# Where the negated head sums stand beside g_h, a smaller head mask, and how the gradient of z reaches all partitions

## The chip, the cores and the metric

The kernel runs on one core of a Trainium2 chip. A core has a matrix engine (TensorE, PE in the profile, with its weight loads PEld), a vector engine (DVE), a scalar engine (ACT), GpSimd (POOL) and a queue engine (SyncE, SP), and 16 DMA engines that all queues share. The metric is the device time of one execution in microseconds; lower is better.

## The reference, cut to what matters

A block of linear attention (no causal mask) with 32 heads of 20 columns (S = 2048 rows, D = 640 columns), followed by a gated MLP with F = 1728, and the gradients of both with respect to the input and all five weights:

```python
def _A_ref(x, wqkv, wo):              # x: [1, 2048, 640], H = 32 heads of Dh = 20
    q, k, v = split(x @ wqkv)
    phi = lambda t: jnp.where(t > 0, t + 1, jnp.exp(t)) + 1e-6
    pq, pk = phi(q), phi(k)
    kv = jnp.einsum("bhsd,bhse->bhde", pk, v)
    z = jnp.einsum("bhsd->bhd", pk)                      # sum of pk over the rows
    num = jnp.einsum("bhqd,bhde->bhqe", pq, kv)
    den = jnp.einsum("bhqd,bhd->bhq", pq, z)[..., None] + 1e-6
    return merge(num / den) @ wo
h  = x + _A_ref(_layernorm(x), A_wqkv, A_wo)
h2 = h + (silu(n @ w1) * (n @ w3)) @ w2                  # n = _layernorm(h)
out, vjp = jax.vjp(...);  grads = vjp(grad_out)          # x, wqkv, wo, w1, w3, w2
```

With r = pq / den, the backward pass needs, for each row and head, sn = the sum over the head's 20 columns of (gradient of num / den) times r. The gradient of z is then a 640-vector: for column d of head h, the sum over all rows of r[row, d] times -sn[row, h]. It is added to the gradient of pk in every row.

## The kernel before, in words

Everything is on one core, in an order written out by hand (a manual schedule; each engine and each DMA queue takes its instructions in program order). Rows are cut into 16 tiles of 128 (`ST = 16`, index t), the 640 columns into 5 blocks of 128 (`DT = 5`, index m). Blocks of 128 columns don't end where heads of 20 columns end: `M_H[m]` is the range of heads that block m touches, (0, 7), (6, 13), (12, 20), (19, 26), (25, 32).

The stages in order of time: the forward attention, the MLP with its backward products, the gradient of w2, then five that matter here.

- The gradient of the MLP's input. For each t, `b_ghn` (L1062) is 54 matmuls; `ln_bwd` (L1077) takes the layer norm's gradient on ACT and DVE and writes row tile t of `g_h`; `b_gT` (L1104) transposes it, `b_gr` (L1120) multiplies by the transposed wo into `gr`, and DVE forms `pb` = gr * r (L1131), sums it by head into `sn` (L1132) and writes -sn as bfloat16 into the 32 columns that stand behind the 640 of `g_h` in the tile `g_hx` (L1133). POOL spreads -sn over the columns of Zb into `sz` (L1135), and `b_gq` (L1137) makes `g_q` from it on DVE.
- `q_parts` (L1143, matmuls at L1155): for each m, r's column block m (the weights) times `g_h` (moving), in two halves j of 320 columns, each summed over 16 row tiles in one PSUM bank. The second half takes 352 columns, so that the 32 columns of -sn are multiplied too; out of these 32 only the heads of block m matter. A list `order` cuts each half into two parts of 8 row tiles; the caller places parts between the last `b_gr` and `b_gq` (L1223 to L1252). At the end of a block m, ACT copies the 640 columns to `qp`, DVE masks the 7 or 8 columns of block m's heads into `gz8` (L1160), and SP transposes `qp` into `QT` (both are parts of the tile `tri`). After the last one DVE sums `gz8` into `gz`, 128 partitions by 5: the gradient of z (L1253).
- `grad_halves` (L1265), shown as `job`: the products for the gradient of wqkv, 16 matmuls of 320 columns each. They are used as filling (`fill(n)`) between short dependent steps. The `q` part's results are written out by POOL's queue.
- The small square products: `gkvT` (L1322) from QT, masked by `masked` (L208); `dwoT`; then five rounds of `square` into `gm` (L1352) with transposes of `gkvT` and one `fill` each. In the first round DVE makes five diagonal 128 x 128 matrices `gzd` from the identity and `gz` (in the tile `small`, L1360). After the fifth, five matmuls of a matrix of ones with these diagonals (L1364) put the 640 values of `gz` on every partition, and two ACT copies (L1367) bring them to `gzb` (128 x 640, float32).
- The gradient of k, for each t: ten matmuls into `dkv` (L1375), DVE adds `gzb` into `gp` (L1378) and multiplies by pk's derivative (L1379). Then the gradient of x (`gxn`, L1429) and those of w1 and w3 (`job` again).

`mask` (L196) holds ones where partition p of block m belongs to head h, repeated over the head's 20 columns: 5 x 8 x 20 bfloat16, 1600 bytes on each partition. `make_mask` (L198) fills it with one DVE memset and two POOL selections for each m while the forward attention runs; `masked` multiplies with it at L211 (eight times in all).

SBUF tiles come from stacks. `mask` lies in the lowest pool, `cp`, that lives to the end, so the tiles of the pools above it, `u1`, `u2` and `bl` (x, all weights, g_h, r, g_q, g_k and so on), start at addresses that depend on its size; those of the other side (`pf`, `ph`, `pa`, `ba`, `br`) do not.

Of the kernel before, what the change touches and what calls it, by code (L numbers as in the profile page):

```python
# [9 lines left out]
P = 128  # L10
BF16 = mybir.dt.bfloat16
F32 = mybir.dt.float32
ALU = mybir.AluOpType
# [5 lines left out]
S, D, H, F = 2048, 640, 32, 1728  # L19
DH = D // H  # L20
ST, DT = S // P, D // P
# [3 lines left out]
HD = D // 2  # L25
# [4 lines left out]
def _heads(lo, hi, g):  # L30
    return lo // g, (hi - 1) // g + 1
# [3 lines left out]
M_H = [_heads(m * P, (m + 1) * P, DH) for m in range(DT)]  # L35
M_MAX = max(b - a for a, b in M_H)
# [19 lines left out]
def kernel(  # L56
# [19 lines left out]
    V, A, T, G, SY = nc.vector, nc.scalar, nc.tensor, nc.gpsimd, nc.sync  # L76
    dma, dmaT, dmaG = SY.dma_start, SY.dma_start_transpose, G.dma_start
# [12 lines left out]
    dram = ctx.enter_context(tc.tile_pool(name="dram", bufs=1, space=bass.MemoryType.DRAM))  # L90
# [5 lines left out]
    w_d = dram.tile([D, D], BF16, name="w_d")  # L96
    kvT_d = dram.tile([D, D], BF16, name="kvT_d")
    dwoT_d = dram.tile([D, D], BF16, name="dwoT_d")
    hn_d = dram.tile([S, D], BF16, name="hn_d")
    hh_d = dram.tile([F, S], BF16, name="hh_d")  # L100
    gg_d = dram.tile([2 * F, S], BF16, name="gg_d")
# [2 lines left out]
    def pool(name, side="left", space=None):  # L104
        kw = dict(space=space) if space is not None else dict(side=side)
        return tc.alloc_tile_pool(name=name, bufs=1, reuse_waits="tile", **kw)

    cp = pool("cp")
# [8 lines left out]
    ident = cp.tile([P, P], BF16, name="ident")  # L117
    make_identity(nc, ident[:])
    ones = cp.tile([P, P], BF16, name="ones")
# [8 lines left out]
    Zb = cp.tile([P, D], BF16, name="Zb")  # L128
# [64 lines left out]
    load_x(3, 4)  # L193
    load_x(4, 8)

    mask = cp.tile([P, DT, M_MAX, DH], BF16, name="mask")  # L196

    def make_mask(m):  # L198
        a, b = M_H[m]
        v = mask[:, m, 0:b - a, :]  # L200
        V.memset(v, 1.0)

        G.affine_select(out=v, in_=v, pattern=[[-DH, b - a], [0, DH]], compare_op=ALU.is_ge, fill=0.0,
                        base=m * P - a * DH, channel_multiplier=1)
        G.affine_select(out=v, in_=v, pattern=[[DH, b - a], [0, DH]], compare_op=ALU.is_gt, fill=0.0,
                        base=a * DH + DH - m * P, channel_multiplier=-1)

    def masked(out, acc, m):  # L208

        a, b = M_H[m]  # L210
        V.tensor_tensor(out=out[:, m, a * DH:b * DH].rearrange("p (h e) -> p h e", e=DH),  # L211
                        in0=acc.rearrange("p (h e) -> p h e", e=DH), in1=mask[:, m, 0:b - a, :], op=ALU.mult)


    w1 = U2.tile([P, DT, FP], BF16, name="w1", tag="A")
# [64 lines left out]
    def two(ap):  # L280
        return ap.rearrange("p (j n) -> p j n", j=2)
# [78 lines left out]
    def heads(ap):  # L360
        return ap.rearrange("p (h e) -> p h e", e=DH)
# [555 lines left out]
    for c in range(SC):  # L917
# [9 lines left out]
        for fc in range(FT):  # L927
# [8 lines left out]
            if c == 0 and fc in (5, 7, 9, 11):  # L936
                a, b = {5: (0, 3), 7: (3, 6), 9: (6, 10), 11: (10, 13)}[fc]
# [12 lines left out]
            if c == SC - 1 and fc in (1, 2, 5, 6):  # L950
                i = (1, 2, 5, 6).index(fc)
# [66 lines left out]
    for fc in range(FT - 1):  # L1018
        b, i = divmod(fc, 4)
        if fc == FT - 2:  # L1020
            gw2_tail()
        acc = ps.tile([P, 2, 512], F32, name="gw", bufs=4)
        for j in range(2):
            for t in range(ST):
                T.matmul(acc[:, j, 0:HD], lhsT=hb[b][:, t, i * P:(i + 1) * P], rhs=g2[:, t, j * HD:(j + 1) * HD],  # L1025
                         start=(t == 0), stop=(t == ST - 1))
# [15 lines left out]


    bl = pool("bl")
    g_hx = bl.tile([P, ST, D + H], BF16, name="g_h")
    g_h = g_hx[:, :, 0:D]
    g_q = bl.tile([P, ST, D], BF16, name="g_q")
    bo = pool("bo")
    r_sb = bo.tile([P, ST, D], BF16, name="r_sb")
    ps = pool("pbp", space=PSUM)  # L1050

    gz8 = cp.tile([P, DT, 8], F32, name="gz8")
    V.memset(gz8[:], 0.0)
    gz = cp.tile([P, DT], F32, name="gz")
# [60 lines left out]
    gr, cc, sz = {}, {}, {}  # L1115

    def per_head(ap):
        return ap.unsqueeze(2).to_broadcast([P, H, DH])

    def b_gr(t):  # L1120

        cc[t] = br.tile([P, D], F32, name="cc")
        V.tensor_tensor(out=heads(cc[t][:]), in0=heads(r_sb[:, t, :]), in1=per_head(rden[:, t, :]), op=ALU.min)
        gr[t] = ps.tile([P, 2, 512], F32, name="gr", bufs=2)
        for j in range(2):
            for c in range(DT):
                T.matmul(gr[t][:, j, 0:HD], lhsT=ghT[t][:, c, :], rhs=wT2[:, c, j * HD:(j + 1) * HD], start=(c == 0),  # L1127
                         stop=(c == DT - 1))
        pb = br.tile([P, D], F32, name="pb")
        sn = br.tile([P, H], F32, name="sn", bufs=2)  # L1130
        V.tensor_tensor(out=two(pb[:]), in0=gr[t][:, :, 0:HD], in1=two(r_sb[:, t, :]), op=ALU.mult)  # L1131
        V.reduce_sum(out=sn[:], in_=heads(pb[:]), axis=AX.X)  # L1132
        V.tensor_scalar(out=g_hx[:, t, D:], in0=sn[:], scalar1=-1.0, scalar2=None, op0=ALU.mult)  # L1133
        sz[t] = br.tile([P, D], F32, name="sz")
        G.tensor_tensor(out=heads(sz[t][:]), in0=heads(Zb[:]), in1=per_head(g_hx[:, t, D:]), op=ALU.mult)  # L1135

    def b_gq(t):  # L1137
        V.tensor_tensor(out=two(sz[t][:]), in0=gr.pop(t)[:, :, 0:HD], in1=two(sz[t][:]), op=ALU.add)
# [4 lines left out]
    def q_parts():  # L1143

        acc = {}
        tags = ("ghn", "ghn", "gr", "ghn", "ghn")
        order = [(0, 0, 0), (0, 0, 1), (1, 0, 0), (1, 0, 1), (0, 8, 0), (1, 8, 0), (2, 0, 0), (2, 0, 1), (0, 8, 1),
                 (1, 8, 1), (2, 8, 0), (2, 8, 1)]
        order += [(m, t0, j) for m in (3, 4) for t0 in (0, 8) for j in range(2)]
        for m, t0, j in order:  # L1150
            if m not in acc:
                acc[m] = ps.tile([P, 2, 512], F32, name="gwo", tag=tags[m], bufs=2)
            n = HD + H * j
            for t in range(t0, t0 + 8):
                T.matmul(acc[m][:, j, 0:n], lhsT=r_sb[:, t, m * P:(m + 1) * P],  # L1155
                         rhs=g_hx[:, t, j * HD:j * HD + n], start=(t == 0), stop=(t == ST - 1))
            if (t0, j) == (8, 1):
                a, b = M_H[m]
                A.copy(out=two(qp[:, m, :]), in_=acc[m][:, :, 0:HD])
                V.tensor_tensor(out=gz8[:, m, 0:b - a], in0=acc.pop(m)[:, 1, HD + a:HD + b], in1=mask[:, m, 0:b - a, 0],  # L1160
                                op=ALU.mult)
                dmaT(out=QT[:, :, m * P:(m + 1) * P], in_=qp[:, m, :])
            yield
# [18 lines left out]
    for t in range(ST):  # L1182
# [14 lines left out]
        if t >= 1:  # L1197
# [3 lines left out]
            if t <= 2 * DT:  # L1201
                n = (t - 1) % DT
# [5 lines left out]
        if u >= 0:  # L1208
            b_gr(u)
# [10 lines left out]
    QT, qp = (tri[:, k * DT:(k + 1) * DT, :] for k in range(2))  # L1220
# [6 lines left out]
    a, b = ST - 1, ST - 2  # L1227
# [23 lines left out]
    load_xnT(2)  # L1251
    part(20)  # L1252
    V.reduce_sum(out=gz[:], in_=gz8[:], axis=AX.X)  # L1253


    OB = DT * D
# [39 lines left out]
    def d_acc():  # L1296
        return ps.tile([P, 2, 512], F32, name="dkv", bufs=3)
# [9 lines left out]
    def unload(acc, out):  # L1307
        for bank, (a, b) in enumerate(((0, SPLIT_D), (SPLIT_D, H))):
            (A.copy, V.tensor_copy)[bank](out=out[:, a * DH:b * DH], in_=acc[:, bank, 0:(b - a) * DH])

    def fill(n):
        for _ in range(n):
            next(jobs, None)
# [4 lines left out]
    for m, (a, b) in enumerate(M_H):  # L1318
        n = (b - a) * DH
        acc = ps.tile([P, 512], F32, name="gkvT", tag="dkv", bufs=3)  # L1320
        for c in range(DT):
            T.matmul(acc[:, 0:n], lhsT=woT[:, c, m * P:(m + 1) * P], rhs=QT[:, c, a * DH:b * DH], start=(c == 0),  # L1322
                     stop=(c == DT - 1))
# [9 lines left out]
    pkT = bv.tile([P, DT, S], BF16, name="pkT")  # L1333
    small = bv.tile([P, ST, D], BF16, name="small", tag="hnN")
    mN, gkv_b, gm = (small[:, n:n + DT] for n in (0, DT, 2 * DT))
    gzd = small[:, 3 * DT, :].rearrange("p (m q) -> p m q", q=P)
    dma(out=mN, in_=m_v)
    dma(out=rows(dwoT_d), in_=dwoT[:])

# [4 lines left out]
        (dma if c < 4 else dmaG)(out=pkb[c][:], in_=pk_v[:, c * 2:(c + 1) * 2, :])  # L1344

    gzb = dx.tile([P, D], F32, name="gzb")
    g_k = gqkv[1] = U1.tile([P, ST, D], BF16, name="g_k", tag="S0")
    for n in range(4):
        load_pk(n)

    for i, (c, ms) in enumerate(SQ_BLOCKS):
        unload(square(wqT[:, 2 * DT:, :], gkvT, i), gm[:, i, :])  # L1352
        tr = ps.tile([P, len(ms), P], BF16, name="trk", tag="dkv", bufs=3)
        for k, m in enumerate(ms):
            T.transpose(tr[:, k, :], gkvT[:, m, c * P:(c + 1) * P], ident[:])
        V.tensor_copy(out=gkv_b[:, c, ms[0] * P:(ms[-1] + 1) * P].rearrange("p (i q) -> p i q", q=P), in_=tr[:])
        fill(1)
        if i == 0:
            for m in range(DT):
                V.tensor_scalar(out=gzd[:, m, :], in0=ident[:], scalar1=gz[:, m:m + 1], scalar2=None, op0=ALU.mult)  # L1360
        dmaT(out=wqT[:, 2 * DT:, i * P:(i + 1) * P], in_=gm[:, i, :])
    acc = d_acc()
    for m in range(DT):
        T.matmul(acc[:, m // 4, m % 4 * P:(m % 4 + 1) * P], lhsT=ones[:], rhs=gzd[:, m, :], start=(m % 4 == 0),  # L1364
                 stop=True, skip_group_check=True)
    for x, y, bank in ((0, 4 * P, 0), (4 * P, D, 1)):
        A.copy(out=gzb[:, x:y], in_=acc[:, bank, 0:y - x])  # L1367

    for t in range(ST):
        c, i = divmod(t, TPC)  # L1370
        u = t // 2
        acc = d_acc()
        for j in range(2):
            for k in range(DT):
                T.matmul(acc[:, j, 0:HD], lhsT=xnT[c][:, k, i * P:(i + 1) * P], rhs=gm[:, k, j * HD:(j + 1) * HD],  # L1375
                         start=(k == 0), stop=(k == DT - 1))
# [7 lines left out]
        if t in (2, 5, 8, 11, 14):  # L1384
            n = t // 3
            acc = square(mN, gkv_b, n)
# [8 lines left out]
        if t in (6, 8, 10, 12):  # L1395
            n = t // 2 - 3
# [110 lines left out]
```

## Time and profile before

| | |
|---|---|
| median of 3 runs | 823.8 us (823.18, 823.80, 824.32) |
| profiled execution, first to last instruction (span) | 821.9 us |
| profiled execution's own time | not recorded apart from the span; the median stands 1.9 us above the span |
| granted TensorE clock | 1.000 |
| PE busy | 814.4 us, 99% of the span, 5522 matmuls |
| DVE, ACT, POOL busy | 453.1, 325.0, 133.1 us |
| DMA | 157.26 MB, mean 191 GB/s |
| q_parts' matmuls (gwo, L1155) | 160, first 537.9, last 563.9 us |
| ones-matmuls for gzb (L1364) | 5, at 582.68 us |

A row of a timeline has the start in us, the time, the engine, the line, the operation, out<-in, how many, and in brackets the idle time before it with what ended it. Matmul durations there overlap (a 320-column matmul is shown with 299 ns, but one starts every 136 ns), so costs on PE are read from the chain of work that ended last, where a stretch of n matmuls has the time from the first start to the next one's. A share of 1.00 or more for DMA means that all 16 engines had packets all the time.

### The profile page before, as it was taken

The numbers are of one execution on the slowest core, as the hardware profiler recorded it, in microseconds if no ns is written. First come the engines' busy times: TensorE is split into PE (matmuls) and PEld (weight loads), VectorE is DVE, ScalarE is ACT, GpSimd is POOL, SyncE is SP. The second block draws the span as 40 slices with busy tenths as digits, with TensorE's granted clock in tenths as the row PEclk, the third lists the DMA queues.
The fourth block names the chain that finished last, engine by engine and source line by source line (L and its number), as shares of the span: only waits on it lengthen the run. The fifth ranks groups of instructions, "written<-read, shape, count | busy, mean of one in ns | idle before, by whom it ended". The sixth has DMA issues, their size and how long they took to land.

```text
span 821.9 us, 14179 instructions
## 1 busy us (share of the span) xinstructions
PE 814.4 (99%) x5522; PEld 522.6 (64%) x5549; DVE 453.1 (55%) x961; ACT 325.0 (40%) x609; POOL 133.1 (16%) x194
## 2 busy tenths in 40 slices
PE   8999999999999999999999999999999999999998
PEld 6677544555555555777777777767777777555554
DVE  7869887999898566300057777772681545200000
ACT  7856688665565666011122212222212334211111
POOL 2243333323223212100001111110220000000000
PEclk9999999999999999999999999999999999999999
DMA  9999889696485556999677897258984898885771
GB/s 233 254 279 227 207 234 312 196 242 157 145 213 155 166 181 162 250 241 267 195 170 179 206 204 188 70 113 178 268 216 93 164 200 181 201 199 137 165 170 38
DMA packets 320883, 157.26 MB, mean 191 GB/s; under 512 B 238704, under 2 KB 314064, under 8 KB 320816
## 3 DMA queue, kind: packets, MB, share of 16 engines
q1 hardware_dynamic: 278768, 115.54, 61.3%
q0 software_dynamic: 7328, 24.48, 8.9%
q10 hardware_dynamic: 34720, 16.34, 8.7%
q8 instruction: 43, 0.70, 0.4%
q14 instruction: 24, 0.20, 0.1%
HBM read 47.01 MB, written 51.13 MB: 119 GB/s over the span
## 4 chain that ended last, share of the span: by engine, by line
PE 94%; DVE 2%; ACT 1%; DMA 1%; issue 0%; SPq 0%; POOL 0%; DVEq 0%; ACTq 0%
PE mm L386 20%; PE job L1271 20%; PE ghn L1070 14%; PE gxn L1429 8%; PE o L833 7%; PE gw L1025 7%; PE gwo L1155 3%; PE big L266 3%; PE gr L1127 3%; PE dkv L1375 3%; PE macc L416 2%; PE at L642 2%; DMA wqkv<-in_A_wqkv_dram 1%; PE dkv L1303 1%; DVE st L147 1%; DMA Wp<-pkx 1%
## 5 line engine op out<-in xcount | busy, mean ns | idle before, releaser
L1271 PE MATMUL job<-gb,hnN 128*128 128x432 bf16 (+2 forms) x656 | 117.0, 342 | 0.0
L1070 PEld LDWEIGHTS <-ggb 128*128 128x128 bf16 x864 | 84.5, 98 | 32.8
L1271 PEld LDWEIGHTS <-hnN 128*128 128x128 bf16 x656 | 63.6, 98 | 53.4
L386 PE MATMUL mm<-pqT,w 128*128 128x512 bf16 x397 | 93.1, 379 | 0.5
L386 PEld LDWEIGHTS <-w 128*128 128x128 bf16 x540 | 52.5, 98 | 63.1 <-issue 0.8
L1275 ACT CAST obs<-job 128x432 bf16<-128x432 f32 (+3 forms) x61 | 29.3, 480 | 123.1 <-PE job L1271 123.1
L833 PE MATMUL o<-w,hhT 128*128 128x320 bf16 x448 | 67.7, 299 | 0.1
L1070 PE MATMUL ghn<-w13a,ggb 128*128 128x320 bf16 x448 | 63.5, 299 | 0.0
L1070 PE MATMUL ghn<-w13b,ggb 128*128 128x320 bf16 x416 | 61.4, 299 | 0.0
L386 PE MATMUL mm<-g2T,w2T 128*128 128x512 bf16 x227 | 58.5, 379 | 0.6
L833 PEld LDWEIGHTS <-hhT 128*128 128x128 bf16 x448 | 43.8, 98 | 23.8 <-issue 0.2
L1025 PE MATMUL gw<-g,hb 128*128 128x320 bf16 x416 | 56.8, 299 | 0.0
L1135 POOL TENSOR_TENSOR sz<-Zb,g_h 128x640 f32<-128x640 bf16 x16 | 20.2, 1260 | 198.8 <-DVE g_h L1133 107.7
L1025 PEld LDWEIGHTS <-hb 128*128 128x128 bf16 x416 | 40.6, 98 | 16.0 <-issue 0.3
L1429 PE MATMUL gxn<-wqT,gT 128*128 128x320 bf16 x320 | 48.7, 299 | 0.0
L406 ACT CAST ghh<-mm 128x512 bf16<-128x512 f32 x48 | 28.3, 590 | 44.7 <-PE mm L386 39.0
L772 ACT ACTIVATE sig<-mm 128x512 bf16<-128x512 f32 x56 | 33.9, 605 | 25.1 <-PE mm L386 21.6
L1082 ACT ACTIVATE gs<-ghn 128x640 bf16<-128x640 f32 x16 | 11.2, 703 | 78.9 <-PE ghn L1070 73.4
L386 PEld LDWEIGHTS <-w2T 128*128 128x128 bf16 x260 | 25.4, 98 | 23.3
L266 PEld LDWEIGHTS <-pqT 128*128 128x128 bf16 x320 | 30.6, 98 | 14.4 <-issue 1.7
L1429 PEld LDWEIGHTS <-gT 128*128 128x128 bf16 x320 | 31.3, 98 | 12.2
L266 PE MATMUL big<-wqkv,pqT 128*128 128x320 bf16 x250 | 38.5, 299 | 0.3
(210 smaller groups left out, 1282.3 us busy)
## 6 DMA issues: line engine op xcount, KB each, us to landing
hh_d<-hhT SPq DMA_DIRECT2D x24, 256.0 KB, 2.8
gg_d<-gate POOLq DMA_DIRECT2D x24, 256.0 KB, 4.1
gg_d<-ghh POOLq DMA_DIRECT2D x24, 256.0 KB, 3.5
ggb<-gg_d SPq DMA_DIRECT2D x6, 896.0 KB, 5.4
ggb<-gg_d ACTq DMA_DIRECT2D x6, 832.0 KB, 5.7
out_dram<-obs ACTq DMA_DIRECT2D x39, 108.0 KB, 3.0
x_sb<-in_A_x_dram SPq DMA_DIRECT2D x6, 640.0 KB, 5.4
ggb<-gg_d SPq DMA_DIRECT2D x2, 1728.0 KB, 13.5
```

The costliest lines, as they stand in the source:

```text
L266: T.matmul(acc, lhsT=pqT[:, c, t * P:(t + 1) * P], rhs=wqkv[:, c, n0:n0 + HD], start=(c == 0), stop=(c == DT - 1))
L386: T.matmul(acc[:], lhsT=w[:, c, fc * P:(fc + 1) * P], rhs=rhs[:, c, :], start=(c == 0), stop=(c == DT - 1))
L406: A.copy(out=ghh[n // 2][:, n % 2, :], in_=acc[:])
L772: A.activation(sig[:, i, :], gp[:], AF.Sigmoid)
L833: T.matmul(o2["ps"][:, 0:HD], lhsT=hhT[c][:, fc, i * P:(i + 1) * P], rhs=w2[:, fc, j * HD:(j + 1) * HD], start=(fc == 0), stop=(fc == FT - 1))
L1025: T.matmul(acc[:, j, 0:HD], lhsT=hb[b][:, t, i * P:(i + 1) * P], rhs=g2[:, t, j * HD:(j + 1) * HD], start=(t == 0), stop=(t == ST - 1))
L1070: T.matmul(acc[:, j, 0:HD], lhsT=ggb[t // 2][:, k, lo:lo + P], rhs=rhs[:, j * HD:(j + 1) * HD], start=(k == 0), stop=(k == NG - 1))
L1127: T.matmul(gr[t][:, j, 0:HD], lhsT=ghT[t][:, c, :], rhs=wT2[:, c, j * HD:(j + 1) * HD], start=(c == 0), stop=(c == DT - 1))
L1155: T.matmul(acc[m][:, j, 0:n], lhsT=r_sb[:, t, m * P:(m + 1) * P], rhs=g_hx[:, t, j * HD:j * HD + n], start=(t == 0), stop=(t == ST - 1))
L1271: T.matmul(acc[:, 0:n], lhsT=lhs[:, t, m * P:(m + 1) * P], rhs=rhs(t), start=(t == 0), stop=(t == ST - 1))
L1275: A.copy(out=ob, in_=acc[:, 0:n])
L1429: T.matmul(acc[:, j, 0:HD], lhsT=g, rhs=wqT[:, k, j * HD:(j + 1) * HD], start=(k == 0), stop=(k == 14))
```

## The change

- `g_hx` gets 16 columns ahead of `g_h`'s 640. The last 13 of them hold -sn of heads 19 to 31 (`n_hi` = 13), written by a second small DVE operation in `b_gr`, after the POOL operation has been queued; the 32 columns behind stay. One row is now 688 elements instead of 672.
- In `q_parts` blocks 0, 1 and 2 take -sn from behind g_h, and only as many columns as their heads reach (7, 13, 20) in the second half; blocks 3 and 4 take it from ahead of g_h (13, 7 columns) in the first half, and their second half has 320.
- `mask` loses the repetition over 20 columns: 80 bytes on each partition. `masked` reads it with a step of 0.
- The diagonals, the five matmuls with ones and the two copies are gone. POOL's queue writes `gz` to a small DRAM tensor `gz_d` (640 separate elements of 4 bytes) and later reads it back to all 128 partitions of `gzb` at once.

```diff
+    gz_d = dram.tile([DT, P], F32, name="gz_d")
...
-    mask = cp.tile([P, DT, M_MAX, DH], BF16, name="mask")
+    mask = cp.tile([P, DT, M_MAX], BF16, name="mask")
...
-        v = mask[:, m, 0:b - a, :]
+        v = mask[:, m, 0:b - a]
         V.memset(v, 1.0)
-        G.affine_select(out=v, in_=v, pattern=[[-DH, b - a], [0, DH]], compare_op=ALU.is_ge, fill=0.0,
+        G.affine_select(out=v, in_=v, pattern=[[-DH, b - a]], compare_op=ALU.is_ge, fill=0.0,
...
-                        in0=acc.rearrange("p (h e) -> p h e", e=DH), in1=mask[:, m, 0:b - a, :], op=ALU.mult)
+                        in0=acc.rearrange("p (h e) -> p h e", e=DH), in1=mask[:, m, 0:b - a].unsqueeze(2).to_broadcast([P, b - a, DH]),
+                        op=ALU.mult)
...
-    g_hx = bl.tile([P, ST, D + H], BF16, name="g_h")
-    g_h = g_hx[:, :, 0:D]
+    G0 = 16
+    g_hx = bl.tile([P, ST, G0 + D + H], BF16, name="g_h")
+    g_h, g_n = g_hx[:, :, G0:G0 + D], g_hx[:, :, G0 + D:]
+    n_hi = H - M_H[3][0]
...
-        V.tensor_scalar(out=g_hx[:, t, D:], in0=sn[:], scalar1=-1.0, scalar2=None, op0=ALU.mult)
+        V.tensor_scalar(out=g_n[:, t, :], in0=sn[:], scalar1=-1.0, scalar2=None, op0=ALU.mult)
         sz[t] = br.tile([P, D], F32, name="sz")
-        G.tensor_tensor(out=heads(sz[t][:]), in0=heads(Zb[:]), in1=per_head(g_hx[:, t, D:]), op=ALU.mult)
+        G.tensor_tensor(out=heads(sz[t][:]), in0=heads(Zb[:]), in1=per_head(g_n[:, t, :]), op=ALU.mult)
+        V.tensor_scalar(out=g_hx[:, t, G0 - n_hi:G0], in0=sn[:, H - n_hi:], scalar1=-1.0, scalar2=None, op0=ALU.mult)
...
-            n = HD + H * j
+            a, b = M_H[m]
+            up, lo = (0, H - a) if m > 2 else (b, 0)
+            x, y = (0, lo + HD) if j == 0 else (lo, lo + HD + up)
             for t in range(t0, t0 + 8):
-                T.matmul(acc[m][:, j, 0:n], lhsT=r_sb[:, t, m * P:(m + 1) * P],
-                         rhs=g_hx[:, t, j * HD:j * HD + n], start=(t == 0), stop=(t == ST - 1))
+                T.matmul(acc[m][:, j, x:y], lhsT=r_sb[:, t, m * P:(m + 1) * P],
+                         rhs=g_hx[:, t, G0 - lo + j * HD + x:G0 - lo + j * HD + y], start=(t == 0), stop=(t == ST - 1))
             if (t0, j) == (8, 1):
-                a, b = M_H[m]
-                A.copy(out=two(qp[:, m, :]), in_=acc[m][:, :, 0:HD])
-                V.tensor_tensor(out=gz8[:, m, 0:b - a], in0=acc.pop(m)[:, 1, HD + a:HD + b], in1=mask[:, m, 0:b - a, 0],
+                A.copy(out=two(qp[:, m, :]), in_=acc[m][:, :, lo:lo + HD])
+                z = acc.pop(m)[:, 0, 0:b - a] if m > 2 else acc.pop(m)[:, 1, HD + a:HD + b]
+                V.tensor_tensor(out=gz8[:, m, 0:b - a], in0=z, in1=mask[:, m, 0:b - a],
                                 op=ALU.mult)
...
     V.reduce_sum(out=gz[:], in_=gz8[:], axis=AX.X)
+    dmaG(out=gz_d[:, :].rearrange("m p -> p m"), in_=gz[:])
...
-    gzd = small[:, 3 * DT, :].rearrange("p (m q) -> p m q", q=P)
...
     gzb = dx.tile([P, D], F32, name="gzb")
+    dmaG(out=gzb[:], in_=gz_d[:, :].rearrange("m p -> (m p)").partition_broadcast(P))
...
-        if i == 0:
-            for m in range(DT):
-                V.tensor_scalar(out=gzd[:, m, :], in0=ident[:], scalar1=gz[:, m:m + 1], scalar2=None, op0=ALU.mult)
         dmaT(out=wqT[:, 2 * DT:, i * P:(i + 1) * P], in_=gm[:, i, :])
-    acc = d_acc()
-    for m in range(DT):
-        T.matmul(acc[:, m // 4, m % 4 * P:(m % 4 + 1) * P], lhsT=ones[:], rhs=gzd[:, m, :], start=(m % 4 == 0),
-                 stop=True, skip_group_check=True)
-    for x, y, bank in ((0, 4 * P, 0), (4 * P, D, 1)):
-        A.copy(out=gzb[:, x:y], in_=acc[:, bank, 0:y - x])
```

More of the change, by code (lines that the diff above doesn't have):

```diff
@@ L194 @@
     load_x(4, 8)
-    mask = cp.tile([P, DT, M_MAX, DH], BF16, name="mask")
+    mask = cp.tile([P, DT, M_MAX], BF16, name="mask")
     def make_mask(m):
         a, b = M_H[m]
-        v = mask[:, m, 0:b - a, :]
+        v = mask[:, m, 0:b - a]
         V.memset(v, 1.0)
-        G.affine_select(out=v, in_=v, pattern=[[-DH, b - a], [0, DH]], compare_op=ALU.is_ge, fill=0.0,
+        G.affine_select(out=v, in_=v, pattern=[[-DH, b - a]], compare_op=ALU.is_ge, fill=0.0,
                         base=m * P - a * DH, channel_multiplier=1)
-        G.affine_select(out=v, in_=v, pattern=[[DH, b - a], [0, DH]], compare_op=ALU.is_gt, fill=0.0,
+        G.affine_select(out=v, in_=v, pattern=[[DH, b - a]], compare_op=ALU.is_gt, fill=0.0,
                         base=a * DH + DH - m * P, channel_multiplier=-1)
```

## The prediction

> **What bounds the kernel now.** First the page: its busy times and its chain of what ended last. (About 0.2% of the time, 1.65 us here, is what a measurement of this kernel can tell from no change.)
>
> ```profile
> PE 814.4 (99%) x5522; PEld 522.6 (64%) x5549; DVE 453.1 (55%) x961; ACT 325.0 (40%) x609; POOL 133.1 (16%) x194
> ...
> PE 94%; DVE 2%; ACT 1%; DMA 1%; issue 0%; SPq 0%; POOL 0%; DVEq 0%; ACTq 0%
> ```
>
> PE is the bound, at a clock of 1.000, and idle for only 7.5 us. So what leaves PE in a dense stretch leaves the time, and what leaves DVE, ACT or POOL is worth nothing unless PE waits for it. Second, the chain in order of time, which gives what PE really pays for a matmul:
>
> ```profile
> 65.21 2.75 PE macc L416 x20
> ...
> 543.41 2.28 PE gwo L1155 x16
> 545.69 1.36 PE gr L1127 x10
> 547.04 17.15 PE gwo L1155 x120
> ...
> 613.03 15.21 PE job L1271 x112
> ```
>
> A 320-column matmul costs 15.21 / 112 = 0.1358 us. The 120 of gwo are 56 of 320 columns and 64 of 352: (17.15 - 56 x 0.1358) / 64 = 0.1492 us, so 32 columns more cost 13.4 ns, 0.417 ns a column, and the stretch holds no idle time. Third, the timeline of the same stretch, for those who come just in time:
>
> ```profile
> 542.95 0.28 PEld L1111 LDWEIGHTS <-g_h 128*128 128x128 bf16 x5 [0.19 <-DVE g_h L1095]
> ...
> 545.26 0.18 DVE L1133 TENSOR_SCALAR g_h<-sn 128x32 bf16<-128x32 f32 x1
> ...
> 545.58 1.26 POOL L1135 TENSOR_TENSOR sz<-Zb,g_h 128x640 f32<-128x640 bf16 x1 [6.60 <-DVE g_h L1133]
> 546.88 0.82 DVE L1138 TENSOR_TENSOR sz<-gr,sz 128x640 f32<-128x640 f32 x1 [1.44 <-POOL sz L1135]
> ...
> 551.04 0.18 DVE L1133 TENSOR_SCALAR g_h<-sn 128x32 bf16<-128x32 f32 x1
> ```
>
> Two gates: PE's transposes wait 0.19 us at 542.95 for DVE's last g_h, and the last -sn (row tile 15) is ready at 551.04 + 0.18 = 551.22. DVE runs without a gap from 538.96 but for the wait on POOL at 546.88, so PE can't hasten this.
>
> Fourth, the timeline where gzb is made, and the rows that price its replacement:
>
> ```profile
> 582.19 0.43 DVE L1309 CAST small<-dkv 128x260 bf16<-128x260 f32 x1 [0.90 <-ACT small L1309]
> ...
> 582.68 0.44 PE L1364 MATMUL dkv<-small,ones 128*128 128x128 bf16 x5
> ...
> 582.96 2.88 PE L1375 MATMUL dkv<-small,xnT 128*128 128x320 bf16 x20
> 583.20 0.76 ACT L1367 COPY gzb<-dkv 128x512 f32<-128x512 f32 x2
> ...
> 584.59 0.82 DVE L1378 TENSOR_TENSOR gp<-dkv,gzb 128x640 f32<-128x640 f32 x1 [1.77 <-PE dkv L1375]
> ```
>
> ```profile
> q1 hardware_dynamic: 278768, 115.54, 61.3%
> q0 software_dynamic: 7328, 24.48, 8.9%
> ```
>
> ```profile
> 564.95 1.20 SPq L1162 DMA_TRANSPOSE tri<-tri  x1
> 574.36 0.54 POOL L1276 DMA_DIRECT2D out_dram<-obs  x1 [4.52 <-ACT obs L1275]
> ```
>
> ```profile
> out_dram<-obs POOLq DMA_DIRECT2D x10, 80.0 KB, 4.4
> pkb<-pk_d SPq DMA_DIRECT2D x4, 320.0 KB, 7.3
> tri<-tri SPq DMA_TRANSPOSE x5, 2.6
> ```
>
> **Part 1, narrower gwo.** Before, 80 matmuls have 32 extra columns: 2560. After, the extra columns of blocks 0 to 4 are 7, 13, 20, 13, 7, in 16 row tiles each: 960. 1600 columns x 0.417 ns = 0.67 us less PE. Not all of it arrives. What is saved before 542.95 (block 0, rows 0 to 7: 8 x 25 columns, 0.08 us) ends in the wait for DVE's g_h, which only grows. Then block 1 (8 x 19 columns, 0.063), block 2 (8 x 12, 0.040) and the first seven of block 0's last part (7 x 25, 0.073) bring PE 0.176 us earlier to the matmul that reads the last -sn. Before, it came there at 546.88 + 16 x 0.1358 + 15 x 0.1492 = 551.29, 0.07 after DVE; after, at 551.11, so it waits until about 551.27. What is left is the rest: that matmul 0.010, block 1 0.063, block 2 0.040, block 3 (512 - 208 = 304 columns) 0.127, block 4 (512 - 112 = 400) 0.167, and 0.02 of margin used up: 0.42 us. The next to be late is the bank that block 3 takes from block 0: free when DVE has masked block 0, about 554.5, wanted at 554.78; no wait.
>
> **Part 2, the negative sums ahead of g_h.** 16 more DVE operations. Nearest rows: L1133 with 32 columns 0.18 us, one-column operations 0.15; I take 0.16, 2.6 us of DVE in all. Behind each on DVE stands either L1085, which waits 1.38 us for ACT, or L1138, which waits 1.44 us for POOL, and POOL's operation is queued ahead of it. Cost nothing; with that cover gone it would be 0.16 us per tile, of which PE would see only tile 14's at the 551.22 gate. That gate waits for L1133, not for the new operation.
>
> **Part 3, odd starts.** Blocks 3 and 4 now read moving columns that start 3 and 9 elements into a row. The nearest row is macc, whose rows of 1284 bytes start at every multiple of 4 bytes: 2.75 / 20 = 0.1375 us with a change of bank among them, against 0.1358. So nothing to 1.7 ns for each of 32 matmuls, below 0.06 us; I take nothing. An odd element is not shown by any row; if the read ran at half rate, the 32 matmuls would cost 16 x (333 + 327) x 0.417 ns = 4.4 us. The Trainium skill ("SBUF — State Buffer", Operand start alignment) says that a bfloat16 operand may start at any multiple of 2 bytes, and that this is about legality and nothing was timed.
>
> **Part 4, gzb by DMA.** PE loses five matmuls: 582.96 - 582.68 = 0.28 us, in a dense stretch, all of it on the path. Next late would be the last part of gm, from DVE at 582.19 + 0.43 = 582.62, before 582.68 and needed only by the fifth matmul: no wait. The two ACT copies (0.76) and five DVE operations (0.90 at 576.49) stood in idle time: nothing. On POOL's queue two DMAs are added. The first waits for gz (DVE, 565.36) and stands ahead of the job results at 567.13; the second stands behind the one at 574.36 and waits for the first to land. Behind both are only result stores, whose ring of ten buffers isn't full, and four pkb loads from 588.65 on. Landing of the second: issued about 574.9, and between 4.4 us (POOL's rows there) and 7.3 us (pkb of the same size at the same time, four in a row), so 579.3 to 582.2; DVE wants it when PE's first dkv is done, about 583.9 in the new time. Hidden with 1.7 us or more. Reading one short line for all partitions has no row.
>
> The first DMA is 640 elements of 4 bytes, 40 for each of 16 engines. Priced by the packet: q1 0.613 x 821.9 x 16 / 278768 = 0.029 us, q0 0.089 x 821.9 x 16 / 7328 = 0.160 us: 1.2 to 6.4 us on each engine from about 566 on. Size speaks for the low end: q0's packets carry 3.3 KB, q1's 0.4 KB. In that time the last transpose into QT (issued 564.95, 2.6 us, so there at 567.6) is due; gkvT's fourth block, at 568.38 + 15 x 0.062 = 569.3, needs it. The margin is 1.7 us: at the low end, hidden. A rule speaks against this part: the Trainium skill ("DMA: Bandwidth & Descriptors", Specifications) puts line rate at 512 bytes and up, with a read-modify-write below. It gives no time for it; if each write cost double the low end, an estimate of 2.4 us would be 0.7 over the margin and the sum 0.7 us later.
>
> **Part 5, mask and addresses.** POOL's ten selections (0.34 to 0.50 us) and DVE's five memsets (0.175) shrink at 42 to 49 us, with their first reader at 66.6: nothing. L211 reads its mask with a step of 0; L1123, which does that already, takes 0.82 us like L1131, which does not: nothing. All tiles of the lower pools move down by 1504 bytes, from 32 bytes past a 64-byte border onto one. What DMAs gain or lose by that, PE sees only where it waits for them: 1.2 us on wqkv at 6.6 and 8.1, and 0.8 us on Wp at 90. After the wqkv waits PE waits for DVE anyhow (L160, at 9.51). So between 0.8 us less (the Wp wait gone) and 0.8 more; I take 0.2 less, as a start on a border should not hurt.
>
> **Sum.** 0.42 + 0.28 + 0.2 = 0.9 us less, span 821.0. The profiled execution's own time is not given apart from its span; the median stands 1.9 us above, so 822.9.
>
> **The rivals.**
> 1. Faster by more than 1.65 us. The sure savings give 0.7; the -sn gate may open too (0.25 more), and the Wp wait and some of wqkv's go (1.0): 821.8. For it: every saving is PE's. Against: only 2.0 us of PE's waits are on DMA. 0.2.
> 2. Slower: the 4-byte writes hold back QT. At 6.4 us an engine instead of 1.2, with the transposes served in turn, QT lands up to 5 us late, 3.3 beyond the margin, in front of gkvT, with everything behind: 823.8 - 0.7 + 3.3 = 826.4. It decides from 1.7 us of lateness on, and for more than 1.65 us of loss from some 4. A late gzb would act alike, but PE has three dkv buffers of 1.4 us in hand there. 0.11.
> 3. Odd starts at half rate: 823.8 - 0.7 + 4.4 = 827.5. 0.03.
> 4. It doesn't pay: the gate at 551.22 or new waits of a few tenths eat part 1, and 0.28 is left: 823.5. 0.12.
>
> The forecast has 0.54. Within 0.2% lie the forecast and rival 4, 0.66; faster rival 1, 0.20; slower 2 and 3, 0.14. The range, 821.5 to 824.9, takes in the forecast, rival 4 and most of rival 1, and leaves out 2 and 3.
>
> **What would show it.** After: gwo in the chain x120 at about 16.6 us with PE idle for some 0.15 us on DVE's L1133 counterpart; no matmuls with ones, dkv following job directly; gp not waiting for DMA; no wait at gkvT; the odd blocks at 0.141 and 0.138 us a matmul. Wrong would be a wait of PE on tri or of DVE on gzb, matmuls near 0.28 us in blocks 3 and 4, or a difference that comes from before 500 us.

## The result, and the profile after

The changed kernel takes 834.05 us (median of 6 runs, 832.77 to 836.04) against 824.08 us for the kernel before (6 runs): a ratio of 1.0121, with an interval of 1.0108 to 1.0134. It is slower by 10 us where 0.9 us of gain was forecast, and lies outside the range. The profiled execution has a span of 833.3 us and a time of its own of 835.05 us, so 1.7 us lie outside the span. Its span is 11.4 us longer than that of before.

The page of the changed kernel, busy times, shares of the chain, and the granted clock in 40 slices of the span:

```profile
PE 818.5 (98%) x5517; PEld 525.9 (63%) x5544; DVE 453.0 (54%) x972; ACT 324.9 (39%) x607; POOL 132.8 (16%) x196
...
PE 95%; DMA 2%; SPq 1%; DVE 1%; ACT 0%; issue 0%; DVEq 0%
...
PEclk9999999999999999999999999997999999999999
```

There are five matmuls fewer, as the change says, yet PE is busy 4.1 us longer: something made matmuls slower, and one slice has a clock of 0.7. In the chain the share of DMA has gone from 1% to 2% and that of SP's queue from 0% to 1%. The chain in order of time shows where:

```profile
547.91 12.45 PE gwo L1162 x88
...
561.10 2.06 SPq L1169
...
565.95 12.52 DMA tri<-tri
...
578.51 1.34 PE gkvT L1330 x10
579.86 1.83 PE dkv L1311 x18
581.69 2.13 PE job L1279 x8
583.83 0.44 PE dkv L1311 x6
584.26 1.09 PE job L1279 x8
585.35 0.33 PE dkv L1311 x6
...
594.58 2.72 PE dkv L1374 x20
```

One transpose into `QT` (a part of `tri`) takes 12.52 us from issue to landing; the prediction's row for these had 2.6. The work behind it then runs at about half rate: eight matmuls of `job` take 2.13 us and, two lines on, 1.09. The chain leaves PE at 560 us because the transposes, not the matmuls, were what `gkvT` waited for.

The timeline (core 0, the same stretch), with the write that the change adds:

```profile
565.73 0.20 DVE L1260 TENSOR_REDUCE gz<-gz 128x5 f32<-128x40 f32 x1
565.95 1.22 SPq L1169 DMA_TRANSPOSE tri<-tri  x1
566.23 0.94 POOL L1261 DMA_DIRECT2D gz_d<-gz  x1 [12.67 <-DVE gz L1260]
...
568.95 1.12 PE L1330 MATMUL gkvT<-tri,woT 128*128 128x140 bf16 x15
...
578.51 1.34 PE L1330 MATMUL gkvT<-tri,woT 128*128 128x140 bf16 x10 [8.44 <-DMA tri<-tri]
```

POOL issues the 640 elements of `gz` at 566.23, between the issue of the last transpose and its landing. The first 15 matmuls of `gkvT` go through; the fourth block waits 8.44 us. The view of the DMA queues from 560 to 582 us gives the time to landing (KB of one, median us):

```profile
out_dram<-obs POOLq DMA_DIRECT2D x2, 80.0 KB, 12.3
...
gz_d<-gz POOLq DMA_DIRECT2D x1, 2.5 KB, 11.7
```

The 2.5 KB took 11.7 us, and the 80 KB job results on the same queue, which took 5.7 us in this stretch before, 12.3 us. The transposes on SP's queue are held up too, so it is not only POOL's queue. The windows (stretch, its length, then busy time of PE, PEld, DVE, ACT and POOL with the number of instructions; the last three numbers are granted clock, DMA share and GB/s):

```profile
570.00:572.00 2.00, 0.07 (x2) 0.00 (x0) 0.39 (x2) 0.00 (x0) 0.41 (x1) 1.00 0.21 18
572.00:574.00 2.00, 0.00 (x0) 0.00 (x0) 0.00 (x0) 0.00 (x0) 0.00 (x0) 0.92 0.80 46
574.00:576.00 2.00, 0.00 (x0) 0.00 (x0) 0.00 (x0) 0.00 (x0) 0.00 (x0) 0.50 0.43 24
576.00:578.00 2.00, 0.00 (x0) 0.00 (x0) 0.00 (x0) 0.00 (x0) 0.00 (x0) 0.50 0.67 37
...
580.00:582.00 2.00, 2.00 (x19) 1.79 (x18) 1.01 (x3) 1.22 (x3) 0.00 (x0) 0.50 1.25 277
...
584.00:586.00 2.00, 2.00 (x23) 1.58 (x21) 0.43 (x1) 1.09 (x3) 0.00 (x0) 1.00 0.00 0
```

While `QT` is awaited the 16 engines move 18 to 46 GB/s, against 119 to 272 in such windows between 566 and 576 us before, and their busy share is 0.21 to 0.80: they are held up without being full of packets. In the window 580 to 582, after the landing, 277 GB/s flow. The clock falls to 0.50 during the wait and stays there until 583.9, 5.4 us after PE has work again.

The 11.4 us come apart as follows (before against after):

- The stretch before the first gwo matmul: 538.09 against 539.02, 0.93 us longer. By the first matmul's own start, which lies some 0.15 us earlier, it is 537.9 before and 538.2 in experiment 2, which keep the old addresses; in the fourteen kernels with the new ones it is 537.6 to 540.2 and once 542.6, with a median of 538.65. So a small loss by the moved tiles is possible here, but single executions scatter by more than that; it stays open how much of the 0.93 us is chance.
- First gwo to first job: 564.20 - 538.09 = 26.11 against 564.77 - 539.02 = 25.75 us: 0.36 less. (The chain has left PE at 564.77; the timeline has the first job matmul at 564.61, and the chain's starts lie 0.16 us behind it.)
- The wait of `gkvT` on `tri`: 8.44 us.
- Work at the half clock: gkvT's last ten 1.34 - 10 x 0.062 = 0.72, then 1.83 - 0.99, 2.13 - 1.09 and 0.44 - 0.33 on dkv, job and dkv (the lower numbers are the same steps of before's chain): 2.7 us.
- The matmuls with ones, gone: from the second job filling to the gradient of k 583.12 - 572.52 = 10.60 against 594.58 - 584.26 = 10.32: 0.28 less.
- From there to the end of the span 238.8 against 238.7.

The sum is 0.93 - 0.36 + 8.44 + 2.7 - 0.28 = 11.4.

### The profile page after: what moved, and what is told of

The parts are those of the page before. It is cut to its first block, busy times and chain, and to the rows that moved or that the text cites. A ratio compares the mean times of both kernels' runs of the same rounds, so it can differ in the third digit from the quotient of the medians.

```text
span 833.3 us, 14182 instructions
## 1 busy us (share of the span) xinstructions
PE 818.5 (98%) x5517; PEld 525.9 (63%) x5544; DVE 453.0 (54%) x972; ACT 324.9 (39%) x607; POOL 132.8 (16%) x196
## 4 chain that ended last, share of the span: by engine, by line
PE 95%; DMA 2%; SPq 1%; DVE 1%; ACT 0%; issue 0%; DVEq 0%
PE mm L388 20%; PE job L1279 19%; PE ghn L1074 14%; PE gxn L1428 8%; PE o L835 7%; PE gw L1027 7%; PE big L268 4%; PE macc L418 3%; PE dkv L1374 3%; PE gr L1131 3%; PE at L644 2%; PE gwo L1162 2%; DMA tri<-tri 2%; PE mm L268 1%; PE dkv L1311 1%; DMA wqkv<-in_A_wqkv_dram 1%
## 5 line engine op out<-in xcount | busy, mean ns | idle before, releaser
L1279 PEld LDWEIGHTS <-g 128*128 128x128 bf16 x320 | 31.4, 99 | 12.0
## 6 DMA issues: line engine op xcount, KB each, us to landing
ggb<-gg_d SPq DMA_DIRECT2D x2, 1728.0 KB, 13.5
```

The lines of the kernel that those rows point to most:

```text
L1279: T.matmul(acc[:, 0:n], lhsT=lhs[:, t, m * P:(m + 1) * P], rhs=rhs(t), start=(t == 0), stop=(t == ST - 1))
```

## The experiments

The theory after the result: the write of 640 separate 4-byte elements to DRAM holds up the DMA traffic for about 12 us, QT's last transpose with it. Rivals were the other parts of the change (the odd starts, the moved tiles), the 640 pieces as a mere number of descriptors, POOL's queue, and the source's layout. Times of single runs are given with their spans; the kernel before had 823.7 to 824.1 us beside them.

**1. The change without the DMA.** Everything is as in the changed kernel, but `gzb` is made with diagonals, ones-matmuls and copies as before. This kernel is the base of most probes below.

```diff
-    dmaG(out=gz_d[:, :].rearrange("m p -> p m"), in_=gz[:])
...
-    dmaG(out=gzb[:], in_=gz_d[:, :].rearrange("m p -> (m p)").partition_broadcast(P))
...
+        if i == 0:
+            for m in range(DT):
+                V.tensor_scalar(out=gzd[:, m, :], in0=ident[:], scalar1=gz[:, m:m + 1], scalar2=None, op0=ALU.mult)
...
+    acc = d_acc()
+    for m in range(DT):
+        T.matmul(acc[:, m // 4, m % 4 * P:(m % 4 + 1) * P], lhsT=ones[:], rhs=gzd[:, m, :], start=(m % 4 == 0),
+                 stop=True, skip_group_check=True)
+    for x, y, bank in ((0, 4 * P, 0), (4 * P, D, 1)):
+        A.copy(out=gzb[:, x:y], in_=acc[:, bank, 0:y - x])
```

> All of the change but the gradient of z by DMA: gzb is made with diagonals, matmuls with ones and two copies again. Theory 1 (the write of 640 elements of 4 bytes holds up the DMA engines, QT's last transpose lands 10 us late and PE waits 8.4 us, then works at half clock for some us): no wait of PE at gkvT, the last transpose into tri lands in 2.6 to 2.7 us, and the time is that of the kernel before less the 0.42 us of the narrower gwo: 823.4, give or take 0.8. Rival 2 (another part, the shifted addresses, the longer rows of g_h or the odd starts, delays the transposes into tri): the wait at gkvT stays and the time is 832 to 836.

Measured: 823.45 us (12 runs) against 823.88 (17 runs), ratio 0.999, interval 0.9978 to 1.0003. Its chain:

```profile
548.01 16.85 PE gwo L1161 x120
564.87 4.35 PE job L1277 x32
569.21 1.56 PE gkvT L1328 x25
```

All 25 matmuls of `gkvT` run in one go, so the wait is gone, and with it the 10 us. The narrower gwo is kept (16.85 us where before had 17.15). So the other parts cost nothing that can be measured and may bring some tenths of a microsecond; the interval doesn't decide that.

**2. The DMA alone.** The kernel before, with only the write and the read in place of diagonals, matmuls and copies.

```diff
+    dmaG(out=gz_d[:, :].rearrange("m p -> p m"), in_=gz[:])
...
+    dmaG(out=gzb[:], in_=gz_d[:, :].rearrange("m p -> (m p)").partition_broadcast(P))
```

> The kernel before with one part of the change alone: gz written to DRAM as 640 elements of 4 bytes and read back to all partitions, no diagonals and no matmuls with ones. Theory 1: last transpose into tri lands after about 12.5 us, PE waits 8 to 9 us at gkvT, then clock 0.5 for some 10 us; 833.5 to 836. Rival 2: no wait there, 823.5.

Measured: 836.29 us (835.64 to 838.96), ratio 1.0148, interval 1.0126 to 1.017. The waits of PE:

```profile
PE gkvT L1324 <- DMA tri<-tri: 10.5, 1, 10.5
```

The whole loss is in this part. The wait (10.5 against 8.4 us) and the landing of `gz_d` (13.5 against 11.7) vary between kernels by some 2 us, and both, with the time, are a little above what was expected.

**3. The write alone, which nobody reads.** On the base of experiment 1.

```diff
+    dmaG(out=gz_d[:, :].rearrange("m p -> p m"), in_=gz[:])
```

> As e1 (gzb by matmuls with ones), with the write of gz to gz_d added in its place; nobody reads it. Theory 1: the write alone does it, although nothing waits for it: landing 11 to 12 us, PE's wait at gkvT 8 to 9 us, 833 to 836. Rival 3 (the read to all partitions, or the wait of POOL between the two, is at fault): no wait at gkvT and 823.4.

Measured: 835.38 us, span 833.6. The DMA view:

```profile
gz_d<-gz POOLq DMA_DIRECT2D x1, 2.5 KB, 12.8
```

PE waits 10.0 us at `gkvT`. Neither the read back nor anyone's waiting for it is needed: the write does it.

**4 and 5. The same 640 elements, 512 bytes apart in DRAM, or into SBUF.** In the first, each element has a row of its own; in the second they go to every second word of an SBUF tile.

```diff
+    gz_w = dram.tile([DT, P, P], F32, name="gz_w")
+    dmaG(out=gz_w[:, :, 0].rearrange("m p -> p m"), in_=gz[:])
...
+    gz_s = cp.tile([P, DT, 2], F32, name="gz_s")
+    dmaG(out=gz_s[:, :, 0], in_=gz[:])
```

> As e3, but the 640 elements are written 512 bytes apart instead of side by side. If the writes queue up because they are parts of the same few DRAM lines (2560 bytes in all), they now land in 3 to 4 us, PE waits less than 1 us at gkvT and the time is 823 to 824.5. If each small write costs its time wherever it goes, landing is again 11 to 12 us and the time 833 to 836.

> As e3 (640 elements of 4 bytes, read by nobody, gzb by matmuls), but written to a tile in SBUF, every second word, instead of DRAM. If it is partial writes to DRAM that cost, the write lands in 2 to 3.5 us, PE waits less than 0.5 us at gkvT, time 823 to 824.5. If it is the number of descriptors, landing is 11 to 14 us, PE waits 8 to 10 us, 833 to 836.

Measured: 825.36 us (span 823.6) and 823.52 us (821.8). The DMA views, of the one and of the other:

```profile
gz_w<-gz POOLq DMA_DIRECT2D x1, 2.5 KB, 4.8
```

```profile
gz_s<-gz POOLq DMA_DIRECT2D x1, 2.5 KB, 3.0
```

As many 4-byte pieces on the same queue at the same time, but 1.2 us of wait at `gkvT` in the one and none in the other, and a clock of 1.00 in both. The second came out as expected for its case; the first is a little dearer than expected (landing 3 to 4 us, a wait below 1 us, at most 824.5 us), so a gap of 512 bytes does not take all of the price away. So it is neither the number of pieces nor the queue nor the reading of `gz`. What counts is where the pieces go: DRAM, and there close together.

**6. Fewer of them.** Two of the five columns, 256 elements side by side.

```diff
+    dmaG(out=gz_d[0:2, :].rearrange("m p -> p m"), in_=gz[:, 0:2])
```

> As e3, but only two of the five columns of gz are written: 256 elements of 4 bytes side by side. If the writes are served one after the other, the 640 took 11.7 to 13.5 us to land, some 2.3 of it fixed, so 15 to 17 ns each, and 256 land in 6 to 7 us: PE waits 3 to 4.5 us instead of 10, the clock may stay at 1.0, time 826.5 to 829. If such a write has a fixed price, landing stays at 11 to 13 us and the time at 833 to 836.

Measured: 834.24 us (span 832.5). The DMA view and the waits:

```profile
gz_d<-gz POOLq DMA_DIRECT2D x1, 1.0 KB, 11.0
```

```profile
PE gkvT L1330 <- DMA tri<-tri: 7.7, 1, 7.7
```

The expectation of a price by the piece (826.5 to 829 us) fell: 40% of the pieces take 11.0 us.

**7. The same 2560 bytes in pieces of 20.** Each partition's five elements stay together, so there are 128 pieces.

```diff
+    gz_p = dram.tile([P, DT], F32, name="gz_p")
+    dmaG(out=gz_p[:, :], in_=gz[:])
```

> As e3, the same 2560 bytes of DRAM, but written as 128 pieces of 20 bytes (the order of the elements is another one; nobody reads them). If the price is by piece, 15 to 17 ns each: landing 4 to 4.8 us, PE waits up to 1.3 us, time 823.5 to 825.5. If it is by byte or by element of 4 bytes, landing is 11 to 13 us, time 833 to 836.

Measured: 823.62 us (span 821.9), no wait at `gkvT`:

```profile
gz_p<-gz POOLq DMA_DIRECT2D x1, 2.5 KB, 2.8
```

This is below the 4 to 4.8 us expected from a price by the piece. Small pieces as such, down to 20 bytes, are harmless here.

**8. The change mended.** `gz` is cast to bfloat16, transposed on PE to 5 x 128 after the first `fill(4)`, and written as five pieces of 512 bytes; the read to all partitions stays as in the change.

```diff
-    dmaG(out=gz_d[:, :].rearrange("m p -> p m"), in_=gz[:])
+    V.tensor_copy(out=gzh[:], in_=gz[:])
...
+    T.transpose(gzt[0:DT, :], gzh[:], ident[:])
+    gzr = cp.tile([P, P], F32, name="gzr")
+    A.copy(out=gzr[0:DT, :], in_=gzt[0:DT, :])
+    dmaG(out=gz_d[:, :], in_=gzr[0:DT, :])
```

> The change with the write mended: gz is rounded to bfloat16 (as the diagonals were), turned by one matmul into 5 partitions of 128, and written as 5 pieces of 512 bytes behind the first four steps of job; the read to all partitions and the narrower gwo stay. If the small pieces were all that was wrong: no wait at gkvT, gp doesn't wait for gzb (landing some 5 us after 575, wanted at 584), and the time is that of e1 less 0.2 us: 823.2 give or take 0.8, ratio 0.999. Rival (the read of one short line by 128 partitions is slow in the crowded stage, too): gp waits and the time is 825 to 828.

Measured: 824.7 us (823.22 to 826.03, 12 runs) against 824.05 (17 runs), ratio 0.9997, interval 0.9984 to 1.001 (the two medians alone would give 1.0008, inside the interval too). The median is above the expected 824.0 at most. The DMA view, and the timeline at `gp`:

```profile
gz_d<-gzr POOLq DMA_DIRECT2D x1, 2.5 KB, 3.2
...
gzb<-gz_d POOLq DMA_DIRECT2D x1, 320.0 KB, 6.7
```

```profile
585.98 0.82 DVE L1383 TENSOR_TENSOR gp<-dkv,gzb 128x640 f32<-128x640 f32 x1 [1.42 <-PE dkv L1380]
```

The read of one line by all partitions lands 6.7 us after its issue, at 583.3, 2.7 us before `gp`, which waits only for PE. So the plan to spread `gz` through DRAM works once the write is in long pieces, but it is no faster than the ones-matmuls by anything this measurement can tell.

**9, 10 and 13. Where it begins: 16, 64 and 32 elements side by side,** on the base of experiment 1.

```diff
+    dmaG(out=gz_d[0:1, 0:16].rearrange("m p -> p m"), in_=gz[0:16, 0:1])
...
+    dmaG(out=gz_d[0:1, 0:64].rearrange("m p -> p m"), in_=gz[0:64, 0:1])
...
+    dmaG(out=gz_d[0:1, 0:32].rearrange("m p -> p m"), in_=gz[0:32, 0:1])
```

> As e3, but only 16 elements of 4 bytes, side by side: 64 bytes of DRAM in all. The 256 of e6 took as long as the 640, so the price is not by the number in all. If it is set by how many pieces fall into one stretch of 64 bytes (16 in e3, e6 and here; one in e4, three to four in e7), landing is again 9 to 12 us, PE waits 6 to 9 us, 831 to 836. If the stretch is 256 or 512 bytes (64 or 128 pieces in e3, 16 here), landing is 3.5 to 5 us and the time 823 to 825. If any such write has a fixed price: 11 us or more.

> As e9 with 64 elements, 256 bytes. Stretch of 64 bytes: as e9, 9 to 12 us. Stretch of 256 bytes: 9 to 12 us here but not in e9. Stretch of 512 bytes: 6 to 7.5 us, PE waits 2 to 4 us, 825 to 828. By the number of elements alone: 3 to 4 us.

> As e9 with 32 elements side by side, 128 bytes. 16 landed in 2.4 us, 64 in 9.2 us. If the pieces in one stretch of 256 bytes are served one after the other, about (9.2 - 2.4) / 48 = 0.14 us each, landing is 4.5 to 5 us, PE waits up to 1.5 us, 823 to 825.5. If only the third and fourth piece of an engine in a stretch make it slow (16 elements are one for each DMA engine, 64 are four), it is 2.4 to 3.5 us or 9 us.

Measured: 823.82, 834.97 and 830.48 us (spans 822.1, 833.3 and 828.8). The DMA views of 16 and 64, and the waits of 32:

```profile
gz_d<-gz POOLq DMA_DIRECT2D x1, 0.1 KB, 2.4
```

```profile
gz_d<-gz POOLq DMA_DIRECT2D x1, 0.2 KB, 9.2
```

```profile
PE gkvT L1330 <- DMA tri<-tri: 4.5, 1, 4.5
```

Sixteen pieces land in 2.4 us, 32 in 8.1 us, 64 in 9.2 us: most of the price comes between 16 and 32 pieces, and 20 times as many as 32 add only 4 to 7 us. If the pieces are dealt out evenly, 32 means a second piece for each of the 16 engines; the trace doesn't show which engine wrote which. Sixteen landed faster than any case expected (3.5 us or more), and 64 as a stretch of 256 bytes that counts as one would (9 to 12 us). That pieces within such a stretch are served one after the other (32 elements at 4.5 to 5 us) fell; 8.1 us lies in neither range that was set out. Experiment 10's time holds 2.3 us of a later start (its first gwo matmul is at 540.2, against 537.9 before) and 6.7 us of wait.

**11. The write through SP's queue,** on the base of experiment 3.

```diff
-    dmaG(out=gz_d[:, :].rearrange("m p -> p m"), in_=gz[:])
+    dma(out=gz_d[:, :].rearrange("m p -> p m"), in_=gz[:])
```

> As e3, all 640 elements side by side, issued by SP's queue instead of POOL's. If the price lies where the writes land, nothing changes: landing 11 to 14 us, PE waits 8 to 10.5 us, 833 to 836. If it is POOL's software queue, landing is 3 to 5 us and the time 823 to 825.5.

Measured: 831.39 us. There is no wait at `gkvT`: on SP's queue the write stands behind QT's transposes, which land in 3.5 us. It is SP's next work that is late, as its timeline shows:

```profile
567.58 11.75 SPq L1185 DMA_TRANSPOSE xnT<-xn_d  x1
```

In place and amount (833 to 836 us, a wait at `gkvT`) the expectation was missed. That the stall goes with the write, and not with POOL's queue, holds: SP is held for 11.75 us by a step that took 3.41 before and 7.94 in the changed kernel; what SP issues next is some 9 us late. PE waits 4.2 us at the square products and then works at the half clock. The profile puts this wait down to DVE; DVE had waited for ACT, and ACT's copy of a job result for 5.5 us on an unknown queue, while POOL's stores of job results took 9.3 us to land. So it is not shown that SP's delay is what PE waited for.

**12. The change with the write issued later,** after dwoT's products, when QT has landed.

```diff
-    dmaG(out=gz_d[:, :].rearrange("m p -> p m"), in_=gz[:])
...
     br.release()
     bo.release()
+    dmaG(out=gz_d[:, :].rearrange("m p -> p m"), in_=gz[:])
```

> The change as it is, with the write issued some 6 us later, behind the last of the dwoT products, when QT has long landed. Theory 1: no wait at gkvT, last transpose into tri 2.6 to 4.6 us; but the write then stands in front of the loads of pkb and of the read of gzb: it lands near 586, gzb near 591, gp waits some 7 us for it on DVE, PE 3 to 7 us for a free dkv buffer: 826 to 831. Rival (the write is harmless once QT is past): 823.2.

Measured: 835.22 us (span 833.5), no better. The waits:

```profile
POOL gzb L1354 <- DMA gz_d<-gz: 14.6, 1, 14.6
...
DVE gp L1377 <- DMA gzb<-gz_d: 13.1, 1, 13.1
...
PE dkv L1310 <- DVE gp L1377: 8.7, 1, 8.7
```

`QT` is in time now, but the read waits 14.6 us for the write, `gp` 13.1 us for the read, and PE 8.7 us for `gp`. Neither of the two places tried hides the write; the expected 826 to 831 us was too hopeful.

**14. The 640 elements, one every 16 bytes.**

```diff
+    gz_w = dram.tile([DT, P, 4], F32, name="gz_w")
+    dmaG(out=gz_w[:, :, 0].rearrange("m p -> p m"), in_=gz[:])
```

> As e3, all 640 elements, one every 16 bytes: 16 pieces in 256 bytes as in e9 instead of 64. If it is the crowding in 256 bytes that counts: landing 4 to 6 us (512 bytes apart took 4.8), PE waits 0.5 to 2.5 us, 823.5 to 826.5. If any two pieces nearer than 512 bytes hinder each other: landing 10 to 14 us, 831 to 836.

Measured: 830.29 us, of which some 4 us lie before 560 us (its first gwo matmul is at 542.6, against 537.9 before), so the time itself, above the expected 823.5 to 826.5, says little. The rows do:

```profile
gz_w<-gz POOLq DMA_DIRECT2D x1, 2.5 KB, 5.3
```

PE waits 2.2 us; this and the landing are as expected if crowding counts, and the landing is nearly that of 512 bytes apart (4.8). A gap of 12 bytes between the elements takes more than half of the price away.

**What stays open.** Shown: the price belongs to 4-byte pieces written side by side to DRAM, from somewhere between 17 and 32 of them on, and it holds up other DMAs, on other queues too. Not shown: why. By the records the time does not pass in the write's own packets: in the changed kernel all of them start between 567.8 and 569.0, and the write's end is signalled at 577.9. Sixteen pieces in 64 bytes, one for each engine if they are dealt out evenly, land in 2.4 us, so engines that share a neighbourhood are not enough; that an engine's second piece lies beside its first would fit 32, 64, 256 and 640 side by side and the two layouts with gaps, but which engine writes which piece is assumed in it. Experiment 7's pieces of 20 bytes lie side by side too and are quick; the trace doesn't show whether they are joined on the way.

## Why the prediction was wrong, point by point

**The step that failed** is in Part 4: the first DMA's "1.2 to 6.4 us on each engine", taken at the low end because "size speaks for the low end", and so hidden with a margin of 1.7 us. Mean packet times of other queues were the wrong measure. Those queues' packets carry 0.4 and 3.3 KB on average; the time from issue to landing of this write is 11.7 us, 9.3 more than that of 16 pieces (2.4), outside both ends, while the records of its own packets look short (16 of 160 bytes, some 0.27 us each). The bound from above was not one: a mean of packets says nothing about what a new kind of write does to the memory and to its neighbours.

**Rival 2 was right in place and sign,** at a chance of 0.11: the write holds back QT, and PE waits on `tri` at gkvT's fourth block. It was not right in how: it had engines busy for 6.4 us with the write's packets and transposes served in turn behind them, where the records show 0.27 us an engine and engines that are not full. Its price, 3.3 us beyond the margin, came out as 8.4 us. It also assumed that PE would go on at full speed afterwards. No step had the clock: 2.7 us of the loss is work at half rate after the wait. A wait on PE was priced at its own length alone.

**The rule set aside.** The Trainium skill ("DMA: Bandwidth & Descriptors", Specifications) names 512 bytes as the size for line rate, with a read-modify-write below; the prediction named it as speaking against this part, and gave an estimate at double the low end, which its sum left out. In direction it was right. In size the runs differ from it both ways: 20-byte pieces landed in 2.8 us and five of 512 bytes in 3.2, while 4-byte pieces took 2.4 to 15.2 us by layout and number.

**Part 1 held.** From the first gwo to the first job 0.36 us was gained, against 0.42 forecast, and 0.35 to 0.37 in experiments 1, 4 and 8 as well. The gate at the last -sn is there, in the timeline of the changed kernel:

```profile
551.97 0.18 DVE L1137 TENSOR_SCALAR g_h<-sn 128x32 bf16<-128x32 f32 x1
552.06 0.17 DVE L1140 TENSOR_SCALAR g_h<-sn 128x13 bf16<-128x13 f32 x1
552.20 12.23 PEld L1162 LDWEIGHTS <-r_sb 128*128 128x128 bf16 x88 [0.20 <-issue]
```

The weight load idles 0.20 us up to 552.20, just after L1137 ends at 552.15; 0.16 was forecast. The profile names no releaser for it ("issue"), so that it is the gate is read from the times. The 16.6 us announced for the x120 stretch are its 17.15 less the 0.52 that the terms of Part 1 take out of it, without the wait; with the forecast wait they are 16.8. It measured 16.85 in experiment 1, the wait included.

**Part 2 held:** the new operation takes 0.17 us (0.16 forecast), and the load at the gate starts before it ends, so it is not what PE waits for. **Part 3 held:** blocks 3 and 4 lie in the x120 stretch; at half rate their 32 matmuls would have added 4.4 us to it, and it got shorter by 0.30 (experiments 1, 4 and 8 have it in one piece). Rival 3 falls. **Part 4's other terms held:** 0.28 us for the ones-matmuls, to the hundredth; and the read's landing, forecast at 4.4 to 7.3 us, was 6.7 us in experiment 8 and 5.3 us in the changed kernel, where it came at 591.9, before `gp` at 596.0.

**Part 5 is not decided.** One reading in it was wrong: the 0.8 us on Wp are 0.2 us of PE and 0.6 us of its weight loads in the same moment, so PE waited 1.4 us on DMA and not 2.0. PE's waits on the early loads shift from kernel to kernel (on wqkv 1.2 us before, 0.5 in the changed kernel, 0.3 in experiment 1, which has another 1.0 us on a transposed input), and the interval of experiment 1 holds both the gain of 0.2 and none. Without the DMA parts, the forecast's terms would be 0.42 + 0.2 = 0.6 us less; experiment 1 has medians 0.43 us apart with an interval of 1.8 us less to 0.2 us more.

What could be measured of the forecast's sum was thus right to a tenth, but for the one term that it bounded from rows of another kind. With 8.4 us of wait and 2.7 us of slow clock behind it, that term decided.

## What to carry to other kernels

Look at a DMA's pieces on the DRAM side before its size: a column-wise store of a few 4-byte values side by side can hold up the DMA traffic of a core for some 10 us, while the same bytes as rows, spread by a gap, or turned on PE first, land in about 3 to 5 us. When a DMA is added beside a chain that lives on other DMAs, price what it does to them, not only its own landing; and when no row of the same kind exists, leave the upper end open rather than take a mean of other packets for it. A wait on PE of more than a few microseconds costs more than its length, because the work after it starts at a lower clock.

## What the runs showed of the hardware that was not expected

Landing of 4-byte writes to DRAM, side by side: 2.4 us for 16, 8.1 for 32, 9.2 for 64, 11.0 for 256, and 11.7 to 15.2 for 640. With a gap: 5.3 us for 640 at 16 bytes, 4.8 at 512 bytes. Into SBUF: 3.0 us. During the slow ones transposes from SBUF to SBUF, on another queue, were held up as well (12.5 us to landing in the changed kernel instead of 2.6), while the engines moved 18 to 46 GB/s.

After waits of PE of 1.2 and 2.2 us the granted clock stayed at 1.00; after one of 4.5 us it was 0.50 for 3.41 us, after 6.7 us (and after experiment 11's 4.2 us, with shorter waits behind it) for 6.83 us, and after 7.7 to 10.5 us for 10.24 us, all multiples of 3.41. In the changed kernel it fell at 573.7, 3.6 us after PE had run dry, and rose 5.4 us after it had work again. The Trainium skill ("TensorE: Matmul & The Clock Gate", Part 1) describes such a gate: half rate after an idle window of about 3.4 us, full rate after a busy one, the windows running free of the kernel. These runs agree with it.
